# Two linear-attention blocks with a gate: the normalised numerator computed token-major and transposed, in place of a feature-major numerator with an expanded reciprocal

## Chip, cores and metric

One core of one Trainium2 chip runs the whole kernel. The metric is the device time of one execution in microseconds; the time before is the median of four runs. The profile is of one further execution, whose span (first to last instruction) is a little shorter than the device time.

## What is computed

Two linear-attention blocks, A and B, read the same input `x` of 2048 tokens by 640 features, with their own weights. There are 32 heads of 20 features. A sigmoid gate per token mixes the two results. Cut to what matters:

```python
# for each block, S = 2048, D = 640, H = 32, Dh = 20
qkv = x @ wqkv                              # 640 -> 3 * 640
phi = lambda t: where(t > 0, t + 1, exp(t)) + 1e-6
pq, pk = phi(q), phi(k)
kv  = einsum("bhsd,bhse->bhde", pk, v)      # per head 20 x 20, over all tokens
z   = einsum("bhsd->bhd", pk)
num = einsum("bhqd,bhde->bhqe", pq, kv)
den = einsum("bhqd,bhd->bhq", pq, z)
o   = num / den
block = o.reshape(B, S, D) @ wo
# the whole
g = sigmoid((x * gate_w).sum(-1))
out = g * A + (1 - g) * B
```

## The kernel before

Names: `P` = 128, `ST` = 16 token tiles of 128, `NS` = 4 groups of 512 tokens, `NQ` = 4 tiles in a group, `NCH` = 512, `DT` = `QT` = 5 feature tiles of 128. All tiles in PSUM come from one pool of eight one-bank buffers; `work` is a pool of two buffers per tag. The gate is multiplied into the reciprocals of the denominators, so that the last projection can add A and B in one accumulation. A matmul's `lhsT` is the stationary operand, its `rhs` the moving one; the contraction runs over partitions.

The queries are computed feature-major (`pqT`: features on partitions, tokens in the free dimension), the keys and values token-major:

```python
def q_group(blk, m, n):          # 128 features x 512 tokens
    pq_ps = ps_tile(f"pq_{blk}")
    for c in range(DT):
        nc.tensor.matmul(pq_ps[:, :NCH], lhsT=Wr[:, c, ...], rhs=xT[:, c, n * NCH:(n + 1) * NCH], ...)
    nc.scalar.activation(out=e[:], in_=pq_ps[:, :NCH], func=ACT.Exp)
    nc.scalar.activation(out=r[:], in_=pq_ps[:, :NCH], func=ACT.Relu)
    nc.vector.scalar_tensor_tensor(out=pqT[:, m, n * NCH:(n + 1) * NCH], in0=e[:], scalar=1.0, in1=r[:], op0=ALU.min, op1=ALU.add)

def kv_chunk(blk, i, with_gate):  # 128 tokens; three PSUM banks p0, p1, p2 of 512, 448 and 320 columns
    for pt, w, off in regions:
        for c in range(DT):
            nc.tensor.matmul(pt[:, :w], lhsT=xT[:, c, sl], rhs=Wr[:, c, off:off + w], ...)
    # ScalarE: Exp of p0 and of 128 columns of p1
    # VectorE: max(., 0) + 1e-6 of the same (kr), then min(e, 1) + r into pk
    # ScalarE: the values from p1 and p2 into vaug
```

`phase_kvwin` contracts `pk` with `vaug` over all tokens and leaves `KVbd`, the per-head 20 x 20 matrices on the diagonal of a 640 x 640 matrix. `den_group` gives the denominators token-major (128 tokens x 32 heads), `rec_ops` their reciprocals times the gate (`recs`). The part that the change replaces makes the reciprocals feature-major by a transpose and an expansion from 32 heads to 640 features with the 0/1 matrix `E`:

```python
def transposes(self, n):         # in RecState
    pr = ps_tile_bf16(f"recT_{self.blk}")
    for q in range(NQ):
        nc.tensor.transpose(out=pr[:H, q * P:(q + 1) * P], in_=self.recs[:, n * NQ + q, :], identity=identb[:])
    nc.vector.tensor_copy(out=self.recT[:H, n * NCH:(n + 1) * NCH], in_=pr[:H, :NCH])

def num_group(blk, oT, recT, j, n):   # 128 features x 512 tokens
    dch = echunks[j]                  # 2 or 3 feature tiles that meet the heads of tile j: 2, 3, 3, 3, 2
    for kk, c in enumerate(dch):
        nc.tensor.matmul(pn[:, :NCH], lhsT=KVbd[:, c, j * P:(j + 1) * P], rhs=pqT[:, c, n * NCH:(n + 1) * NCH], ...)
    nc.tensor.matmul(pr[:, :NCH], lhsT=E[:, j * P:(j + 1) * P], rhs=recT[:, n * NCH:(n + 1) * NCH], start=True, stop=True)
    nc.scalar.copy(out=numsb[:], in_=pn[:, :NCH])
    nc.vector.tensor_tensor(out=oT[:, j, n * NCH:(n + 1) * NCH], in0=numsb[:], in1=pr[:, :NCH], op=ALU.mult)

def final_group(i):                   # 128 tokens: ten stationary tiles (five of oTA, five of oTB), two banks of 320 columns
    for kk, (oT, wo, j) in enumerate(steps):
        nc.tensor.matmul(o0[:, :FH], lhsT=oT[:, j, sl], rhs=wo[:, j, 0:FH], ...)
        nc.tensor.matmul(o1[:, :FH], lhsT=oT[:, j, sl], rhs=wo[:, j, FH:D], ...)
    # ScalarE copies o0, VectorE o1, then the output DMA
```

The order of the whole is: q and kv of A interleaved; `KVbd`, denominators and reciprocals of A; four kv chunks of B; all transposes and numerators of A; q and kv of B interleaved; `KVbd`, denominators of B (three groups of 512 tokens); the last five q groups of B; numerators of B for group 0; then for each group of 512 tokens its B numerators (from group 1 on) and its four output chunks. Tile's scheduler may draw ready instructions ahead.

Of the kernel before, what the change touches and what calls it, by code (L numbers as in the profile page):

```python
# [8 lines left out]
P = 128  # L9
FP32 = mybir.dt.float32  # L10
BF16 = mybir.dt.bfloat16
ACT = mybir.ActivationFunctionType
ALU = mybir.AluOpType
# [3 lines left out]
def kernel(  # L17
# [11 lines left out]
    nc = tc.nc  # L29
# [3 lines left out]
    S, D = x2.shape  # L33
    H = 32
    Dh = D // H
    assert D % H == 0 and D % P == 0 and S % P == 0
    DT = D // P
    ST = S // P
    NCH = min(512, S)
    assert S % NCH == 0 and NCH % P == 0  # L40
    NS = S // NCH
    NQ = NCH // P
    QT = D // P
# [19 lines left out]
    for c in range(DT):  # L63
        h_lo = (c * P) // Dh
        h_hi = ((c + 1) * P - 1) // Dh
# [7 lines left out]
    echunks = []  # L73
# [7 lines left out]
    persist = ctx.enter_context(tc.tile_pool(name="persist", bufs=1))  # L81
    consts = ctx.enter_context(tc.tile_pool(name="consts", bufs=1))
    work = ctx.enter_context(tc.tile_pool(name="work", bufs=2))
    psum = ctx.enter_context(tc.tile_pool(name="psum", bufs=8, space=bass.MemoryType.PSUM))

    def ps_tile_bf16(name):
        return psum.tile([P, 2 * NCH], BF16, tag="ps", name=name)

    def ps_tile(name):
        return ps_tile_bf16(name).bitcast(FP32)  # L90
# [5 lines left out]
    pqT = persist.tile([P, QT, S], BF16, name="pqT")  # L96
    pk = persist.tile([P, ST, D], BF16, name="pk")
    vaug = persist.tile([P, ST, VAUG_W], BF16, name="vaug")
    oTA = persist.tile([P, QT, S], BF16, name="oTA")
    oTB = persist.tile([P, QT, S], BF16, name="oTB")  # L100
    KVbd = persist.tile([P, DT, D], BF16, name="KVbd")
    ZselA = persist.tile([P, DT, H], BF16, name="ZselA")
    ZselB = persist.tile([P, DT, H], BF16, name="ZselB")
    recTA = persist.tile([P, S], BF16, name="recTA")
    recTB = persist.tile([P, S], BF16, name="recTB")
    recsA = persist.tile([P, ST, H], BF16, name="recsA")
    recsB = persist.tile([P, ST, H], BF16, name="recsB")

# [10 lines left out]
        out=E[:H], in_=E[:H], pattern=[[-1, D]], compare_op=ALU.is_ge, fill=0.0, base=Dh - 1,  # L119
        channel_multiplier=Dh,  # L120
    )
    nc.vector.memset(recTA[:], 0.0)
    nc.vector.memset(recTB[:], 0.0)
    nc.gpsimd.memset(  # L124
        vaug[:].rearrange("p i (h t) -> p i h t", t=Dh + 1)[:, :, :, Dh:Dh + 1], 1.0
    )
# [60 lines left out]
    def q_group(blk, m, n):  # L187
        pq_ps = ps_tile(f"pq_{blk}")
        for c in range(DT):
            nc.tensor.matmul(  # L190
                pq_ps[:, :NCH],
                lhsT=Wr[:, c, OFF_Q + m * P:OFF_Q + (m + 1) * P],
                rhs=xT[:, c, n * NCH:(n + 1) * NCH],
                start=(c == 0), stop=(c == DT - 1),
            )
        e = work.tile([P, NCH], BF16, tag="qe", name="qe")
        r = work.tile([P, NCH], BF16, tag="qr", name="qr")
        nc.scalar.activation(out=e[:], in_=pq_ps[:, :NCH], func=ACT.Exp)  # L198
        nc.scalar.activation(out=r[:], in_=pq_ps[:, :NCH], func=ACT.Relu)  # L199
        nc.vector.scalar_tensor_tensor(  # L200
            out=pqT[:, m, n * NCH:(n + 1) * NCH], in0=e[:], scalar=1.0, in1=r[:],
            op0=ALU.min, op1=ALU.add,
        )

    def kv_chunk(blk, i, with_gate: bool):
        nB = K1_W + V0_W
        nC = V1_W + (1 if with_gate else 0)
        sl = slice(i * P, (i + 1) * P)
        p0 = ps_tile(f"p0_{blk}")
        p1 = ps_tile(f"p1_{blk}")  # L210
        p2 = ps_tile(f"p2_{blk}")
        regions = [(p0, K0_W, OFF_K0), (p1, nB, OFF_K1), (p2, nC, OFF_V1)]
        for pt, w, off in regions:
            for c in range(DT):
                first, last = (c == 0), (c == DT - 1)
                nc.tensor.matmul(pt[:, :w], lhsT=xT[:, c, sl], rhs=Wr[:, c, off:off + w], start=first, stop=last)  # L216
        e = work.tile([P, D], BF16, tag="ke", name="ke")
        r = work.tile([P, D], BF16, tag="kr", name="kr")
        nc.scalar.activation(out=e[:, 0:K0_W], in_=p0[:, 0:K0_W], func=ACT.Exp)  # L219
        nc.scalar.activation(out=e[:, K0_W:D], in_=p1[:, 0:K1_W], func=ACT.Exp)  # L220
        nc.vector.tensor_scalar(r[:, 0:K0_W], p0[:, 0:K0_W], 0.0, 1e-6, op0=ALU.max, op1=ALU.add)
        nc.vector.tensor_scalar(r[:, K0_W:D], p1[:, 0:K1_W], 0.0, 1e-6, op0=ALU.max, op1=ALU.add)
        nc.vector.scalar_tensor_tensor(  # L223
            out=pk[:, i, :], in0=e[:], scalar=1.0, in1=r[:], op0=ALU.min, op1=ALU.add,
        )
        nc.scalar.copy(
            out=vaug[:, i, 0:VSPLIT_H * (Dh + 1)].rearrange("p (h t) -> p h t", t=Dh + 1)[:, :, 0:Dh],
            in_=p1[:, K1_W:K1_W + V0_W].rearrange("p (h t) -> p h t", t=Dh),
        )
        nc.scalar.copy(  # L230
            out=vaug[:, i, VSPLIT_H * (Dh + 1):VAUG_W].rearrange("p (h t) -> p h t", t=Dh + 1)[:, :, 0:Dh],
            in_=p2[:, 0:V1_W].rearrange("p (h t) -> p h t", t=Dh),
        )
        if with_gate:
            nc.scalar.activation(out=gexp[:, i:i + 1], in_=p2[:, nC - 1:nC], func=ACT.Exp, scale=-1.0)
# [31 lines left out]

    class RecState:

        def __init__(self, blk, Zsel, gc, recs, recT):  # L270
            self.blk = blk
            self.Zsel = Zsel
            self.gc = gc
            self.recs = recs
            self.recT = recT
            self.den_tiles = [ps_tile(f"den{n}_{blk}") for n in range(NS)]

        def den_group(self, i):
# [16 lines left out]
                op=ALU.mult,  # L295
            )

        def transposes(self, n):
            pr = ps_tile_bf16(f"recT_{self.blk}")
            for q in range(NQ):  # L300
                i = n * NQ + q
                nc.tensor.transpose(out=pr[:H, q * P:(q + 1) * P], in_=self.recs[:, i, :], identity=identb[:])
            nc.vector.tensor_copy(out=self.recT[:H, n * NCH:(n + 1) * NCH], in_=pr[:H, :NCH])

    def num_group(blk, oT, recT, j, n):
        dch = echunks[j]
        pn = ps_tile(f"num_{blk}")
        pr = ps_tile(f"rt_{blk}")
        for kk, c in enumerate(dch):
            nc.tensor.matmul(  # L310
                pn[:, :NCH], lhsT=KVbd[:, c, j * P:(j + 1) * P], rhs=pqT[:, c, n * NCH:(n + 1) * NCH],
                start=(kk == 0), stop=(kk == len(dch) - 1),
            )
        nc.tensor.matmul(  # L314
            pr[:, :NCH], lhsT=E[:, j * P:(j + 1) * P], rhs=recT[:, n * NCH:(n + 1) * NCH],
            start=True, stop=True,
        )
        numsb = work.tile([P, NCH], BF16, tag="numsb", name="numsb")
        nc.scalar.copy(out=numsb[:], in_=pn[:, :NCH])  # L319
        nc.vector.tensor_tensor(  # L320
            out=oT[:, j, n * NCH:(n + 1) * NCH], in0=numsb[:], in1=pr[:, :NCH], op=ALU.mult,
        )

    FH = D // 2

    def final_group(i):
        sl = slice(i * P, (i + 1) * P)
        o0 = ps_tile("o0")
        o1 = ps_tile("o1")
        steps = [(oTA, woA, j) for j in range(QT)] + [(oTB, woB, j) for j in range(QT)]  # L330
        for kk, (oT, wo, j) in enumerate(steps):
            first, last = (kk == 0), (kk == len(steps) - 1)
            nc.tensor.matmul(o0[:, :FH], lhsT=oT[:, j, sl], rhs=wo[:, j, 0:FH], start=first, stop=last)  # L333
            nc.tensor.matmul(o1[:, :FH], lhsT=oT[:, j, sl], rhs=wo[:, j, FH:D], start=first, stop=last)  # L334
        osb = work.tile([P, D], BF16, tag="osb", name="osb")
        nc.scalar.copy(out=osb[:, 0:FH], in_=o0[:, :FH])  # L336
        nc.vector.tensor_copy(out=osb[:, FH:D], in_=o1[:, :FH])  # L337
        nc.sync.dma_start(out=out2[sl, :], in_=osb[:])
# [21 lines left out]
            kv_chunk("A", arg, True)  # L360
    phase_gate()
    phase_kvwin("A", ZselA)
    recA = RecState("A", ZselA, gcol, recsA, recTA)
    for i in range(ST):
        recA.den_group(i)
    for n in range(NS):
# [3 lines left out]
    LEAD_KV = min(ST, 4)  # L370
    for i in range(LEAD_KV):
        kv_chunk("B", i, False)
    for n in range(NS):
        recA.transposes(n)
    for n in range(NS):
        for j in range(QT):
            num_group("A", oTA, recTA, j, n)
    q_items_B = [("q", (n, m)) for n in range(NS - 1) for m in range(QT)]
    kv_items_B = [("kv", i) for i in range(LEAD_KV, ST)]
    for kind, arg in interleave(kv_items_B, q_items_B):  # L380
        if kind == "q":
            q_group("B", arg[1], arg[0])
        else:
            kv_chunk("B", arg, False)
    phase_kvwin("B", ZselB)
    recB = RecState("B", ZselB, gcolB, recsB, recTB)
    for i in range((NS - 1) * NQ):
        recB.den_group(i)
    for n in range(NS - 1):
        recB.rec_ops(n)  # L390
    for m in range(QT):
        q_group("B", m, NS - 1)
    for n in range(NS - 1):
        recB.transposes(n)
    if NS > 1:
        for j in range(QT):
            num_group("B", oTB, recTB, j, 0)
    for i in range((NS - 1) * NQ, ST):
        recB.den_group(i)
    recB.rec_ops(NS - 1)  # L400
    for n in range(NS):
        if n == NS - 1:
            recB.transposes(n)
        if n > 0 or NS == 1:
            for j in range(QT):
                num_group("B", oTB, recTB, j, n)
        for q in range(NQ):
            final_group(n * NQ + q)


# [28 lines left out]
```

## Time and profile before

| | before |
|---|---|
| device time, median of 4 runs | 241.11 us (240.51 to 242.0) |
| span of the profiled execution | 239.3 us |
| TensorE busy | 227.0 us, 95% |
| VectorE busy | 137.1 us, 57% |
| ScalarE busy | 127.7 us, 53% |
| matmuls | 1511 |

How to read it: matmuls are pipelined, so the duration of one (379 ns for 512 columns) is longer than the distance from one start to the next. The cost of a matmul in a row of matmuls is that distance, which the chain of work that ended last shows by its merged pieces. Idle time of an engine that is not the bottleneck costs nothing. Line numbers such as L310 are those of the kernel; L310 are the numerator matmuls, L314 the expansion of the reciprocal, L302 the transposes of the reciprocals.

### The profile page before, as it was taken

What the parts mean: (1) busy time and instruction counts of PE and PEld (TensorE: products, weight loads), DVE (VectorE), ACT (ScalarE), POOL (GpSimd) and SP (SyncE); (2) the same over time, 40 slices, a digit from 0 to 9 for tenths busy, and PEclk for the clock granted to TensorE, in tenths of its full rate; (3) what the DMA queues carried; (4) which work ended last, traced back from release to release, by engine and by line L of the source; (5) the groups of instructions that cost most, each with busy time, mean ns of one, the idle gap of its engine ahead of it and who ended that gap; (6) DMA issues with size and microseconds to landing.
All of it is one profiled execution on the core that took longest, in us unless ns stands there. A gap on an engine that the chain in (4) does not pass through costs nothing.

```text
span 239.3 us, 3842 instructions
## 1 busy us (share of the span) xinstructions
PE 227.0 (95%) x1511; PEld 129.5 (54%) x1511; DVE 137.1 (57%) x256; ACT 127.7 (53%) x281; POOL 8.0 (3%) x12
## 2 busy tenths in 40 slices
PE   0599999999999999999999999999999999999994
PEld 0235555455555975544554555559547657576572
DVE  3456656575657488888665656564884252432511
ACT  2047676867776326677668677763581242421410
POOL 8400000000000000000000000000000000000000
PEclk9999999999999999999999999999999999999999
DMA  6999700000000910000000000000000101101011
GB/s 186 187 283 198 272 0 1 1 3 0 0 0 9 358 49 0 3 0 1 0 4 0 0 0 3 0 0 3 0 4 27 55 30 55 55 30 55 27 56 58
DMA packets 18786, 12.05 MB, mean 50 GB/s; under 512 B 11600, under 2 KB 18768, under 8 KB 18768
## 3 DMA queue, kind: packets, MB, share of 16 engines
q1 hardware_dynamic: 18768, 11.80, 18.0%
q8 instruction: 12, 0.20, 0.3%
q14 instruction: 6, 0.05, 0.1%
HBM read 6.55 MB, written 2.62 MB: 38 GB/s over the span
## 4 chain that ended last, share of the span: by engine, by line
PE 94%; POOL 3%; DVE 1%; POOLq 0%; issue 0%; DVEq 0%
PE p_A L216 18%; PE p_B L216 18%; PE pq_A L190 10%; PE o L334 9%; PE o L333 9%; PE pq_B L190 9%; PE num_A L310 5%; PE num_B L310 5%; PE rt_B L314 2%; PE rt_A L314 2%; PE kva_A L249 1%; PE kva_B L249 1%; PE pb L184 1%; POOL KVbd L127 1%; POOL vaug L124 1%; PE kvb_B L249 1%
## 5 line engine op out<-in xcount | busy, mean ns | idle before, releaser
L216 PEld LDWEIGHTS <-xT 128*128 128x128 bf16 x480 | 46.7, 97 | 43.5
L200 DVE SCALAR_TENSOR_TENSOR pqT<-qe,qr 128x512 bf16<-128x512 bf16 x40 | 27.6, 690 | 40.7 <-ACT qr L199 40.7
L216 PE MATMUL p_B<-Wr,xT 128*128 128x512 bf16 (+2 forms) x240 | 45.7, 343 | 0.0
L216 PE MATMUL p_A<-Wr,xT 128*128 128x512 bf16 (+2 forms) x240 | 45.4, 344 | 0.0
L190 PEld LDWEIGHTS <-Wr 128*128 128x128 bf16 x200 | 19.9, 100 | 20.9 <-issue 2.9
L223 DVE SCALAR_TENSOR_TENSOR pk<-ke,kr 128x640 bf16<-128x640 bf16 x32 | 26.4, 824 | 1.1
L337 DVE CAST osb<-o 128x320 bf16<-128x320 f32 x16 | 7.9, 491 | 32.7 <-PE o L334 30.1
L336 ACT CAST osb<-o 128x320 bf16<-128x320 f32 x16 | 6.8, 425 | 37.0 <-PE o L333 37.0
L190 PE MATMUL pq_A<-xT,Wr 128*128 128x512 bf16 x100 | 25.5, 400 | 0.0
L190 PE MATMUL pq_B<-xT,Wr 128*128 128x512 bf16 x100 | 24.0, 379 | 0.0
L333 PE MATMUL o<-woB,oTB 128*128 128x320 bf16 x80 | 22.2, 299 | 0.0
L334 PE MATMUL o<-woA,oTA 128*128 128x320 bf16 x80 | 22.2, 299 | 0.0
L334 PE MATMUL o<-woB,oTB 128*128 128x320 bf16 x80 | 22.2, 299 | 0.0
L333 PE MATMUL o<-woA,oTA 128*128 128x320 bf16 x80 | 22.2, 299 | 0.0
L198 ACT ACTIVATE qe<-pq_A 128x512 bf16<-128x512 f32 x20 | 11.9, 597 | 16.7 <-PE pq_A L190 16.7
L198 ACT ACTIVATE qe<-pq_B 128x512 bf16<-128x512 f32 x20 | 11.9, 597 | 11.5 <-PE pq_B L190 11.5
L310 PEld LDWEIGHTS <-KVbd 128*128 128x128 bf16 x104 | 9.9, 98 | 11.3
L320 DVE TENSOR_TENSOR oTB<-numsb,rt_B 128x512 bf16<-128x512 bf16 x20 | 13.5, 685 | 3.8 <-ACT numsb L319 3.1
L320 DVE TENSOR_TENSOR oTA<-numsb,rt_A 128x512 bf16<-128x512 bf16 x20 | 13.6, 687 | 2.0 <-ACT numsb L319 0.9
L310 PE MATMUL num_B<-pqT,KVbd 128*128 128x512 bf16 x52 | 14.5, 379 | 0.0
L310 PE MATMUL num_A<-pqT,KVbd 128*128 128x512 bf16 x52 | 14.5, 379 | 0.0
L219 ACT ACTIVATE ke<-p_B 128x512 bf16<-128x512 f32 x16 | 9.6, 597 | 9.1 <-PE p_B L216 9.1
(73 smaller groups left out, 254.3 us busy)
## 6 DMA issues: line engine op xcount, KB each, us to landing
out_dram<-osb SPq DMA_DIRECT2D x16, 160.0 KB, 1.8
Wr<-in_A_wqkv_dram SPq DMA_DIRECT2D x3, 800.0 KB, 6.1
Wr<-in_B_wqkv_dram SPq DMA_DIRECT2D x3, 800.0 KB, 6.3
woA<-in_A_wo_dram SPq DMA_DIRECT2D x1, 800.0 KB, 5.9
woB<-in_B_wo_dram SPq DMA_DIRECT2D x1, 800.0 KB, 7.4
xT<-in_A_x_dram SPq DMA_TRANSPOSE x10, 4.2
Wr<-in_gate_w_dram SPq DMA_DIRECT2D x1, 1.2 KB, 7.7
```

What stands on the lines that cost most here:

```text
L190: nc.tensor.matmul(pq_ps[:, :NCH], lhsT=Wr[:, c, OFF_Q + m * P:OFF_Q + (m + 1) * P], rhs=xT[:, c, n * NCH:(n + 1) * NCH], start=(c == 0), ...
L198: nc.scalar.activation(out=e[:], in_=pq_ps[:, :NCH], func=ACT.Exp)
L200: nc.vector.scalar_tensor_tensor(out=pqT[:, m, n * NCH:(n + 1) * NCH], in0=e[:], scalar=1.0, in1=r[:], op0=ALU.min, op1=ALU.add,)
L216: nc.tensor.matmul(pt[:, :w], lhsT=xT[:, c, sl], rhs=Wr[:, c, off:off + w], start=first, stop=last)
L219: nc.scalar.activation(out=e[:, 0:K0_W], in_=p0[:, 0:K0_W], func=ACT.Exp)
L223: nc.vector.scalar_tensor_tensor(out=pk[:, i, :], in0=e[:], scalar=1.0, in1=r[:], op0=ALU.min, op1=ALU.add,)
L310: nc.tensor.matmul(pn[:, :NCH], lhsT=KVbd[:, c, j * P:(j + 1) * P], rhs=pqT[:, c, n * NCH:(n + 1) * NCH], start=(kk == 0), stop=(kk == len ...
L314: nc.tensor.matmul(pr[:, :NCH], lhsT=E[:, j * P:(j + 1) * P], rhs=recT[:, n * NCH:(n + 1) * NCH], start=True, stop=True,)
L320: nc.vector.tensor_tensor(out=oT[:, j, n * NCH:(n + 1) * NCH], in0=numsb[:], in1=pr[:, :NCH], op=ALU.mult,)
L333: nc.tensor.matmul(o0[:, :FH], lhsT=oT[:, j, sl], rhs=wo[:, j, 0:FH], start=first, stop=last)
L334: nc.tensor.matmul(o1[:, :FH], lhsT=oT[:, j, sl], rhs=wo[:, j, FH:D], start=first, stop=last)
L337: nc.vector.tensor_copy(out=osb[:, FH:D], in_=o1[:, :FH])
```

## The change

The numerator is computed token-major, like the denominator: a 128-token tile of `pqT` becomes the stationary operand and the columns of `KVbd` that belong to its heads move through. Six pieces per chunk, of 140, 140, 80, 80, 140 and 140 columns, fill two banks of 320 columns (16 heads each). The reciprocal then has the same layout, tokens on partitions and heads in the free dimension, and is applied while the bank is evicted, by a multiplication that broadcasts it over the 20 features of a head. Neither the transposed reciprocal nor its expansion is needed any more. The result `oN` is token-major, and the output projection wants features on partitions, so it is transposed on TensorE, 20 transposes for 512 tokens, and copied out of PSUM by ScalarE and VectorE in turn.

The order changes too: eight of B's kv chunks are put between the chunks of A's numerator, one after every second; B's first chunks are put between the last q groups; and each output chunk of one group of 512 tokens follows a numerator chunk of the next group.

The diff, cut to its core:

```diff
-    recTA = persist.tile([P, S], BF16, name="recTA")
-    recTB = persist.tile([P, S], BF16, name="recTB")
...
-    nc.vector.memset(recTA[:], 0.0)
-    nc.vector.memset(recTB[:], 0.0)
...
-        def transposes(self, n): ...
-    def num_group(blk, oT, recT, j, n): ...
...
+    # o_pieces: [c, u, v, bank, start, stop], columns u:v of feature tile c; a window that crosses FH = 320 is cut there
+    def o_chunk(blk, i, recs, oN):
+        q = i % NQ
+        po = [ps_tile(f"o0_{blk}"), ps_tile(f"o1_{blk}")]
+        lhsT = pqT[:, :, i * P:(i + 1) * P]
+        for (c, u, v, bank, st, sp) in o_pieces:
+            base = 0 if bank == 0 else FH
+            nc.tensor.matmul(
+                po[bank][:, u - base:v - base], lhsT=lhsT[:, c], rhs=KVbd[:, c, u:v], start=st, stop=sp,
+                skip_group_check=True,
+            )
+        nh0 = FH // Dh
+        nc.vector.tensor_tensor(
+            out=oN[:, q, 0:FH].rearrange("p (h t) -> p h t", t=Dh),
+            in0=po[0][:, 0:FH].rearrange("p (h t) -> p h t", t=Dh),
+            in1=recs[:, i, 0:nh0, None].to_broadcast([P, nh0, Dh]),
+            op=ALU.mult,
+        )
+        nc.vector.tensor_tensor(   # the same for columns FH:D from po[1]
...
+    def o_transposes(blk, n, oN, oT):
+        for j in range(QT):
+            pt = ps_tile_bf16(f"oT_{blk}")
+            for q in range(NQ):
+                nc.tensor.transpose(
+                    out=pt[:, q * P:(q + 1) * P], in_=oN[:, q, j * P:(j + 1) * P], identity=identb[:],
+                )
+            if j % 2 == 0:
+                nc.scalar.copy(out=oT[:, j, n * NCH:(n + 1) * NCH], in_=pt[:, :NCH])
+            else:
+                nc.vector.tensor_copy(out=oT[:, j, n * NCH:(n + 1) * NCH], in_=pt[:, :NCH])
...
     for i in range(LEAD_KV):
         kv_chunk("B", i, False)
+    kv_next = LEAD_KV
     for n in range(NS):
-        recA.transposes(n)
-    for n in range(NS):
-        for j in range(QT):
-            num_group("A", oTA, recTA, j, n)
+        oN = work.tile([P, NQ, D], BF16, tag="oN", name="oN")
+        for q in range(NQ):
+            o_chunk("A", n * NQ + q, recsA, oN)
+            if q % 2 == 1:
+                kv_chunk("B", kv_next, False)
+                kv_next += 1
+        o_transposes("A", n, oN, oTA)
...
+    oN = work.tile([P, NQ, D], BF16, tag="oN", name="oN")
     for m in range(QT):
+        if m < NQ:
+            o_chunk("B", m, recsB, oN)
         q_group("B", m, NS - 1)
-    for n in range(NS - 1):
-        recB.transposes(n)
-    if NS > 1:
-        for j in range(QT):
-            num_group("B", oTB, recTB, j, 0)
+    o_transposes("B", 0, oN, oTB)
     for i in range((NS - 1) * NQ, ST):
         recB.den_group(i)
     recB.rec_ops(NS - 1)
     for n in range(NS):
-        if n == NS - 1:
-            recB.transposes(n)
-        if n > 0 or NS == 1:
-            for j in range(QT):
-                num_group("B", oTB, recTB, j, n)
+        if n + 1 < NS:
+            oN = work.tile([P, NQ, D], BF16, tag="oN", name="oN")
         for q in range(NQ):
+            if n + 1 < NS:
+                o_chunk("B", (n + 1) * NQ + q, recsB, oN)
             final_group(n * NQ + q)
+        if n + 1 < NS:
+            o_transposes("B", n + 1, oN, oTB)
```

More of the change, by code (lines that the diff above doesn't have):

```diff
@@ L268, with __init__ @@
     class RecState:
-        def __init__(self, blk, Zsel, gc, recs, recT):
+        def __init__(self, blk, Zsel, gc, recs):
             self.blk = blk
@@ L274, in __init__ @@
             self.recs = recs
-            self.recT = recT
             self.den_tiles = [ps_tile(f"den{n}_{blk}") for n in range(NS)]
@@ L296, in rec_ops @@
             )
-        def transposes(self, n):
-            pr = ps_tile_bf16(f"recT_{self.blk}")
-            for q in range(NQ):
[L301 to L322, printed above, removed]
@@ L324 @@
-    FH = D // 2
+    FH = (H // 2) * Dh
+    assert FH % Dh == 0
+    o_pieces = []
+    prev_hi = 0
+    bank_started = [False, False]
+    for c in range(DT):
+        h_lo = (c * P) // Dh
+        h_hi = ((c + 1) * P - 1) // Dh
+        lo, hi = h_lo * Dh, (h_hi + 1) * Dh
+        ranges = [(lo, hi)]
+        for (a, b) in ranges:
+            for (u, v) in ((a, min(b, FH)), (max(a, FH), b)):
+                if u < v:
+                    bank = 0 if u < FH else 1
+                    o_pieces.append([c, u, v, bank, not bank_started[bank], False])
+                    bank_started[bank] = True
+        prev_hi = hi
@@ new lines @@
+    assert prev_hi == D
+    for bank in range(2):
+        idxs = [k for k, pc in enumerate(o_pieces) if pc[3] == bank]
+        o_pieces[idxs[-1]][5] = True
+    def o_chunk(blk, i, recs, oN):
[16 more added lines that the diff above has]
+        nc.vector.tensor_tensor(
+            out=oN[:, q, FH:D].rearrange("p (h t) -> p h t", t=Dh),
+            in0=po[1][:, 0:D - FH].rearrange("p (h t) -> p h t", t=Dh),
+            in1=recs[:, i, nh0:H, None].to_broadcast([P, H - nh0, Dh]),
+            op=ALU.mult,
+        )
@@ new lines, in o_transposes @@
+    def o_transposes(blk, n, oN, oT):
+        for j in range(QT):
+            pt = ps_tile_bf16(f"oT_{blk}")
+            for q in range(NQ):
+                nc.tensor.transpose(
+                    out=pt[:, q * P:(q + 1) * P], in_=oN[:, q, j * P:(j + 1) * P], identity=identb[:],
+                )
+            if j % 2 == 0:
+                nc.scalar.copy(out=oT[:, j, n * NCH:(n + 1) * NCH], in_=pt[:, :NCH])
+            else:
+                nc.vector.tensor_copy(out=oT[:, j, n * NCH:(n + 1) * NCH], in_=pt[:, :NCH])
@@ L326, in final_group, with o_block @@
+    def o_block(blk, n, recs, oT):
+        oN = work.tile([P, NQ, D], BF16, tag="oN", name="oN")
+        for q in range(NQ):
+            o_chunk(blk, n * NQ + q, recs, oN)
+        o_transposes(blk, n, oN, oT)
     def final_group(i):
@@ L362 @@
     phase_kvwin("A", ZselA)
-    recA = RecState("A", ZselA, gcol, recsA, recTA)
+    recA = RecState("A", ZselA, gcol, recsA)
     for i in range(ST):
@@ L372 @@
         kv_chunk("B", i, False)
+    kv_next = LEAD_KV
     for n in range(NS):
-        recA.transposes(n)
-    for n in range(NS):
-        for j in range(QT):
-            num_group("A", oTA, recTA, j, n)
+        oN = work.tile([P, NQ, D], BF16, tag="oN", name="oN")
[5 more added lines that the diff above has]
+        o_transposes("A", n, oN, oTA)
     q_items_B = [("q", (n, m)) for n in range(NS - 1) for m in range(QT)]
-    kv_items_B = [("kv", i) for i in range(LEAD_KV, ST)]
+    kv_items_B = [("kv", i) for i in range(kv_next, ST)]
     for kind, arg in interleave(kv_items_B, q_items_B):
@@ L385 @@
     phase_kvwin("B", ZselB)
-    recB = RecState("B", ZselB, gcolB, recsB, recTB)
+    recB = RecState("B", ZselB, gcolB, recsB)
     for i in range((NS - 1) * NQ):
@@ L401 @@
     for n in range(NS):
-        if n == NS - 1:
-            recB.transposes(n)
-        if n > 0 or NS == 1:
-            for j in range(QT):
-                num_group("B", oTB, recTB, j, n)
+        if n + 1 < NS:
+            oN = work.tile([P, NQ, D], BF16, tag="oN", name="oN")
         for q in range(NQ):
+            if n + 1 < NS:
+                o_chunk("B", (n + 1) * NQ + q, recsB, oN)
             final_group(n * NQ + q)
+        if n + 1 < NS:
+            o_transposes("B", n + 1, oN, oTB)
 _INS = ['A_x', 'A_wqkv', 'A_wo', 'B_x', 'B_wqkv', 'B_wo', 'gate_w']
```

## The prediction

> **What bounds the kernel now.** I read the page first: busy time per engine, then the slices, then the chain that ended last.
>
> ```profile
> PE 227.0 (95%) x1511; PEld 129.5 (54%) x1511; DVE 137.1 (57%) x256; ACT 127.7 (53%) x281; POOL 8.0 (3%) x12
> ...
> PEclk9999999999999999999999999999999999999999
> ...
> PE 94%; POOL 3%; DVE 1%; POOLq 0%; issue 0%; DVEq 0%
> ```
>
> The reader is to see one bound: TensorE (PE) holds 94% of the chain, at full clock in every slice. Nothing else is near it on average, so what counts is TensorE time added and removed, and whether another engine becomes the bound inside a stage. The next view is the chain in order of time, for the A numerator stage and the work around it.
>
> ```profile
> 82.10 2.08 PE kvb_A L249 x32
> ...
> 85.02 1.60 PE den_A L281 x64
> 86.62 10.41 PE p_B L216 x58
> 97.03 1.00 PE recT_A L302 x16
> 98.03 0.54 PE num_A L310 x2
> 98.56 0.22 PE rt_A L314
> 98.78 0.65 PE num_A L310 x3
> ...
> 113.46 0.22 PE rt_A L314
> 113.67 2.71 PE p_B L216 x15
> ```
>
> Columns: start, length, instructions. These rows are my price list, because a matmul's own duration (379 ns at 512 columns) overlaps with the next; the step is what it costs. A 512-column matmul steps 0.65/3 = 0.216 us, a 147-column one 2.08/32 = 0.065, a 32-column one 1.60/64 = 0.025, a 128-column transpose 1.00/16 = 0.062. A key and value chunk (p_B, 15 matmuls) takes 2.71. All of these except the rt matmul load a new 128-column stationary operand (the transpose one of 32 columns), so weight loads are already inside these steps: at 0.025 us they do not show.
>
> The stage windows (length, then each engine's busy time) and the groups that the change replaces or copies:
>
> ```profile
> 97.03:113.67 16.64, 16.64 (x89) 7.98 (x90) 14.60 (x24) 12.05 (x22) 0.00 (x0) 1.00 0.01 1
> ...
> 162.37:174.69 12.32, 12.32 (x167) 9.07 (x165) 8.38 (x21) 5.46 (x11) 0.00 (x0) 1.00 0.00 1
> ```
>
> ```profile
> L319 ACT CAST numsb<-num_A 128x512 bf16<-128x512 f32 x20 | 11.7, 585 | 4.6 <-PE num_A L310 3.8 <-DVE oTA L320 0.5
> ...
> L337 DVE CAST osb<-o 128x320 bf16<-128x320 f32 x16 | 7.9, 491 | 32.7 <-PE o L334 30.1 <-ACT osb L336 2.6
> ...
> L303 DVE COPY recTA<-recT_A 32x512 bf16<-32x512 bf16 x4 | 1.4, 403 | 0.0
> ...
> L261 DVE TENSOR_TENSOR KVbd<-kva_A,BD 128x140 bf16<-128x140 f32 x2 | 0.6, 296 | 0.0
> ```
>
> In the A numerator window TensorE is fully busy, VectorE 14.60 of 16.64 us, ScalarE 12.05. VectorE has little room in this stage even now.
>
> **What the Trainium skill says.** "TensorE: Matmul & The Clock Gate", section "Wait — 56ns, not 53.3ns?", gives start-to-start as N/2.4 GHz plus about 2.5 ns at full clock: 216 ns for 512 columns, 56 for 128. The trace agrees: 0.216, and 0.065 at 147 columns where the rule says 0.064. The same page, section "Back-to-back issue gap", says that streams of weight load and matmul sustain only about 81 ns at 128 columns; this trace contradicts it, since 147 columns with a fresh weight load each step 65 ns. I price by the trace. "VectorE: DVE Perf Modes", section "The perf-mode tier table", puts a two-tensor operation with a PSUM operand at one element per cycle and a copy from PSUM at up to two. The trace agrees: 296 ns for the 140-element product from PSUM, 403 for the 512-element bf16 copy against 685 for the 512-element product. "PSUM — Partial Sum Buffer", section "Specifications (TRN2)", gives eight banks per partition; the kernel's PSUM pool has eight one-bank buffers, and the trace of before shows no wait for one among its longer waits.
>
> **The change part by part.**
>
> Removed on TensorE, per block: 52 numerator matmuls and 20 expansions of the reciprocal, all of 512 columns, and 16 transposes of reciprocals. For A this is 97.03 to 113.67, 16.64 us. For B the chain has four pieces: 174.69 to 179.47 (4.78), 190.83 to 194.72 (3.89), 205.59 to 209.46 (3.87), and the last from about 220.35 to 224.92 (4.57), in which TensorE also waits some 0.6 us for the copy of the transposed reciprocals (recTB). Together 17.1; both blocks 33.75 us.
>
> Added on TensorE, per 128-token chunk: six matmuls with a pqT tile as stationary operand, whose column windows follow the heads: 140, 140, 80, 80, 140, 140. From the 0.065 step less 2.9 ns per seven columns I put 140 columns at 0.062 and 80 at 0.037, so 4 x 0.062 + 2 x 0.037 = 0.322 us. Two blocks of 16 chunks: 32 x 0.322 = 10.3. This is where the saving comes from: the numerator streamed 13 x 512 columns per 512 tokens and the expansion 5 x 512, 9,216 in all; now it is 4 x 720 = 2,880. Then 20 transposes per 512 tokens, 160 in all; I take 0.060, between the 0.062 read above and the page's 0.056: 9.6. Sum added 19.9.
>
> TensorE alone: 33.75 - 19.9 = 13.9 us less, 241.1 - 13.9 = 227.2.
>
> Moved: VectorE now evicts the numerator itself, two products of 320 elements per chunk (485 to 490 ns each, from the 491 of the osb eviction of the same size), and ScalarE's 585 ns numerator casts go. The transposed result is evicted by copies, three by ScalarE (585) and two by VectorE (403). Also, eight B key and value chunks are moved in between A's chunks. For 512 tokens of A, TensorE takes 4 x 0.322 + 2 x 2.71 + 20 x 0.060 = 7.9 us. VectorE takes 8 x 0.49 for the products, 2 x (0.686 + 0.282 + 0.824) for the two key chunks, 2 x 0.403 for copies: 3.9 + 3.6 + 0.8 = 8.3 by durations. But VectorE's instructions overlap at their ends: in the timeline a 686 ns operation of the key chunk is followed after 0.61. Taking 0.07 off each of the products, and about that off some others, gives about 7.5. So VectorE is at 95 to 100% of TensorE's pace for 32 us. ScalarE has 2 x 1.74 + 3 x 0.585 = 5.2, no bound.
>
> Near balance with chained waits does not run without gaps. At the end of each 512 tokens, five PSUM buffers hold transposes, the next two chunks want four, and only three are free until a copy is done; ScalarE's copies queue behind value casts, which wait for VectorE. Working one period through by hand, the second chunk of the next period waits 0.2 to 0.5 us. I charge 0.35 x 4 = 1.4 us.
>
> B's entry: three denominators' reciprocals keep VectorE busy about 3.5 us (168.96 to 172.4 in the timeline), and four chunks of products (8 x 0.42 = 3.4) plus five q operations (0.69 each, 3.4) follow. TensorE has only five q groups of 1.08 and four chunks of 0.322, 6.7 us from about 169.7, so it reaches the transposes near 176.4, while VectorE has evicted the fourth chunk near 177.5. Up to 1.1 us of wait, partly filled if the next chunks are scheduled ahead; I charge 0.6. In the later B stages VectorE has half its time free, and each transpose stage is followed by ten A matmuls of the output projection (1.36 us), which cover its copies: nothing charged. The two VectorE memsets at the start lie off the chain, which there runs through POOL: nothing gained.
>
> Sum: 227.2 + 1.4 + 0.6 = 229.2; I say 229.
>
> **The rivals.** First, **weight loads come to light**: a weight load is recorded at 97 ns, and 192 short matmuls and 160 transposes at 97 each make 34.1 us against 33.75 removed, so about 241.5 and no change. For it speaks that 80 columns stream in less time than a load lasts, and the skill's 81 ns; against it, the denominator's 0.025 us steps with full-width loads. I give it little. Second, **VectorE becomes the bound of the A stage**: if its durations add without overlap and chained waits leave gaps of 10%, a period is 9.1 us and not 7.9, which costs 4.9 and ends near 233. For it speaks 8.3 against 7.9; against it, the overlap seen and the quieter q stage behind, in which VectorE catches up. Third, **TensorE alone**: buffers hide all of it and the schedule fills B's entry, 227; transposes at 0.056 would then give 226.6. In before, VectorE ran at 88% in that same stage without stopping TensorE.
>
> **Range and chances.** The centre is TensorE's sum plus 2 us of waits. Below it lie the 2 us of waits not occurring and 0.6 from the transposes; above it the second rival's 4 us. So 225.5 to 233.5. Faster by over 2% means under 236.3: to miss it, waits of over 9 us or the first rival are needed; I give faster 0.94, same 0.05, slower 0.01.
>
> **What would show it.** In the profile after, the chain should still be some 90% TensorE; six-matmul chunks should step about 0.32 us and twenty transposes 1.2; the products should be near 490 ns and alternate with key operations, with VectorE over 90% busy in a window some 33 us long from 97; small TensorE waits should be charged to VectorE or ScalarE evictions at the boundaries of the 512 tokens, about 0.35 each. The prediction is wrong if transposes or short matmuls step near 97 ns, if the products with a broadcast operand take much more than 490, or if the A stage with its eight key chunks takes over 36 us.

## The result, and the profile after

The changed kernel takes 227.57 us (median of ten runs, 226.88 to 228.22) against 241.43 for the kernel before: a ratio of 0.943, 95% interval 0.9413 to 0.9448. The prediction said 229.0, and 225.5 to 233.5 as the range.

The page of the changed kernel: busy times, the granted clock, the chain that ended last by engine.

```profile
PE 213.4 (94%) x1687; PEld 133.4 (59%) x1687; DVE 137.2 (61%) x286; ACT 116.1 (51%) x265; POOL 8.0 (4%) x12
...
PEclk9999999999999999999999999999999999999999
...
PE 90%; DVE 3%; POOL 3%; ACT 1%; POOLq 0%; issue 0%; DVEq 0%; ACTq 0%
```

TensorE is still the bound, with 176 more matmuls in 13.6 us less busy time. Some of the chain has gone to VectorE and ScalarE (3% and 1%), and the rest of this page is about where. The same chain in order of time, through one group of 512 tokens of A:

```profile
97.55 0.63 PE o_A L321 x12
98.18 2.71 PE p_B L212 x15
100.89 0.63 PE o_A L321 x12
101.52 2.71 PE p_B L212 x15
104.23 1.12 PE oT_A L343 x20
105.34 0.63 PE o_A L321 x12
```

Every piece starts where the last one ended: two numerator chunks 0.63 us (0.315 each), twenty transposes 1.12 (0.056 each), no gap at the boundary from transposes to the next chunks. The windows of the changed kernel, A's numerator stage and then B's entry (length, then the busy time of TensorE, weight loads, VectorE, ScalarE, GpSimd):

```profile
97.55:128.73 31.18, 31.18 (x297) 21.12 (x295) 29.52 (x65) 18.55 (x44) 0.00 (x0) 1.00 0.01 2
...
161.07:172.07 11.00, 10.89 (x151) 7.33 (x147) 10.51 (x25) 6.66 (x13) 0.00 (x0) 1.00 0.01 1
```

A's stage is TensorE from end to end, although VectorE is busy for 95% of it. At B's entry VectorE is busy for 96% and the chain runs through it:

```profile
161.93 0.41 PE den_B L276 x16
...
162.35 1.77 DVE rcp L285 x2
...
164.38 0.95 DVE rcp L285
165.33 0.34 DVE oN L326
...
165.87 0.40 DVE oN L332
166.27 0.60 DVE pqT L196
```

To compare kernels without the start, I take two stretches from the first start of the matmuls that contract keys and values (kva): A's, from kva_A to kva_B, holds A's numerators and all of B's projections but the last five q groups; B's runs from kva_B to the end of the span.

| | A's stretch | B's stretch | span |
|---|---|---|---|
| before | 83.5 | 77.1 | 239.3 |
| changed | 76.4 | 70.3 | 225.9 |
| 1 new arithmetic, old order | 82.7 | 75.6 | 237.5 |
| 2 old arithmetic, new order | 83.5 | 83.4 | 245.1 |
| 3 the change in A alone | 76.4 | 78.1 | 232.7 |
| 4 copies on VectorE | 76.8 | 70.5 | 226.8 |
| 5 copies on ScalarE | 77.1 | 70.1 | 226.4 |
| 6 numerator pieces twice | 81.4 | 75.1 | 235.2 |
| 7 transposes twice | 80.8 | 74.6 | 233.6 |
| 8 reciprocals later | 76.3 | 69.9 | 225.9 |
| 9 old arithmetic, new order in A | 83.5 | 77.1 | 239.5 |
| 10 as 8, memsets moved | 76.4 | 69.6 | 223.5 |

The change saves 7.1 us in A's stretch and 6.8 in B's. The start gave none of it: kva_A begins at 78.7 us before and 79.2 after, and between 78.2 and 79.7 in other runs whose start is that of one of these two (the last section says what moves it). B's stretch ends with the last output's eviction and transfer, which lie behind TensorE's last matmul: 3.5 to 3.9 us in these executions, but 4.6 in run 3. Up to the start of that matmul B takes 73.28 us before and 66.32 changed.

### The profile page after: what moved, and what is told of

Same layout as the page of the kernel before. It is cut to its first block, busy times and chain, and to the rows that moved or that the text cites. A ratio compares the mean times of both kernels' runs of the same rounds, so it can differ in the third digit from the quotient of the medians.

```text
span 225.9 us, 4153 instructions
## 1 busy us (share of the span) xinstructions
PE 213.4 (94%) x1687; PEld 133.4 (59%) x1687; DVE 137.2 (61%) x286; ACT 116.1 (51%) x265; POOL 8.0 (4%) x12
## 4 chain that ended last, share of the span: by engine, by line
PE 90%; DVE 3%; POOL 3%; ACT 1%; POOLq 0%; issue 0%; DVEq 0%; ACTq 0%
PE p_A L212 19%; PE p_B L212 19%; PE pq_A L186 11%; PE o L364 10%; PE o L365 10%; PE pq_B L186 7%; PE o_A L321 2%; PE oT_A L343 2%; PE o_B L321 2%; PE oT_B L343 1%; PE kva_B L245 1%; PE kva_A L245 1%; PE pb L180 1%; DVE rcp L285 1%; POOL KVbd L123 1%; POOL vaug L120 1%
## 5 line engine op out<-in xcount | busy, mean ns | idle before, releaser
L186 PE MATMUL pq_A<-xT,Wr 128*128 128x512 bf16 x100 | 26.0, 406 | 0.0
L186 PE MATMUL pq_B<-xT,Wr 128*128 128x512 bf16 x100 | 23.0, 379 | 0.0
L364 PE MATMUL o<-woA,oTA 128*128 128x320 bf16 x80 | 21.8, 299 | 0.1
L365 PE MATMUL o<-woA,oTA 128*128 128x320 bf16 x80 | 21.8, 299 | 0.0
L194 ACT ACTIVATE qe<-pq_B 128x512 bf16<-128x512 f32 x20 | 11.9, 597 | 10.2 <-DVE rcp L285 7.3
L217 DVE TENSOR_SCALAR kr<-p_B 128x512 bf16<-128x512 f32 x16 | 11.0, 689 | 4.3 <-ACT ke L215 4.3
L217 DVE TENSOR_SCALAR kr<-p_A 128x512 bf16<-128x512 f32 x16 | 11.0, 686 | 3.9 <-ACT ke L215 3.9
L321 PEld LDWEIGHTS <-pqT 128*128 128x128 bf16 x192 | 11.6, 98 | 1.8
L195 ACT ACTIVATE qr<-pq_A 128x512 bf16<-128x512 f32 x20 | 11.8, 592 | 0.0
L195 ACT ACTIVATE qr<-pq_B 128x512 bf16<-128x512 f32 x20 | 11.8, 591 | 0.0
```

The lines of the kernel that those rows point to most:

```text
L186: nc.tensor.matmul(pq_ps[:, :NCH], lhsT=Wr[:, c, OFF_Q + m * P:OFF_Q + (m + 1) * P], rhs=xT[:, c, n * NCH:(n + 1) * NCH], start=(c == 0), ...
L321: nc.tensor.matmul(po[bank][:, u - base:v - base], lhsT=lhsT[:, c], rhs=KVbd[:, c, u:v], start=st, stop=sp, skip_group_check=True,)
```

## The experiments

The theory after the result: TensorE's sum sets the time, and the new order is what lets it, by putting other matmuls beside the evictions. The rivals: the arithmetic alone brings the gain; the order alone brings it; VectorE's near balance costs something in A.

**1. The changed arithmetic in the order of before.**

```diff
     for n in range(NS):
-        oN = ...; for q: o_chunk("A", ...); after every second one kv_chunk("B", kv_next, False)
-        o_transposes("A", n, oN, oTA)
+        o_block("A", n, recsA, oTA)          # four chunks, then their transposes
 ...
     for m in range(QT):
-        if m < NQ: o_chunk("B", m, recsB, oN)
         q_group("B", m, NS - 1)
-    o_transposes("B", 0, oN, oTB)
+    o_block("B", 0, recsB, oTB)
 ...                                          # and o_block("B", n, ...) ahead of each group's outputs
```

> The changed arithmetic in the order of before: all of A's numerator in one stretch, each B numerator group in one stretch ahead of its four output chunks. Theory (TensorE's saving is paid out only because the new order puts other matmuls beside the evictions): VectorE needs about 8 x 0.40 + 2 x 0.35 = 3.9 us for 512 tokens and TensorE only 4 x 0.315 + 1.12 = 2.4, so TensorE waits about 1.5 us in each of A's four groups and up to 2.4 us in each of B's; 235 to 241 us. Rival (the arithmetic alone brings the gain, buffers and the scheduler hide the evictions): 226.5 to 229.

Measured: 239.3 us, ratio to the kernel before 0.9918 (0.9892 to 0.9944). The new arithmetic by itself brings about 2 of the 13.9 us. Its chain in A's numerator stage:

```profile
98.36 0.40 DVE oN L326
...
101.15 0.40 DVE oN L332
101.54 0.80 DVE oTA L349 x2
...
111.90 0.41 DVE oN L326
112.36 0.40 PE oT_A L343 x4
```

Not one TensorE piece stands in it for 14 us: eight products at 0.40 and two copies, 3.98 us for 512 tokens, where TensorE has 2.4 us of work. The stage's window says the same, VectorE 15.77 of 15.80 us:

```profile
97.30:113.10 15.80, 14.60 (x174) 9.93 (x173) 15.77 (x41) 5.44 (x11) 0.00 (x0) 1.00 0.01 2
```

Here the page's average misleads: VectorE is 58% busy over the span and is the bound of this stage. TensorE's "busy" 14.60 is no evidence against it either; that count includes short matmuls whose records reach over the waits (a transpose is recorded at 219 ns and steps 56). The stage took 16.64 us before, so TensorE's saving turned into a wait for VectorE. In B each group's transposes wait in the same manner (B's stretch is 75.6).

**2. The arithmetic of before in the new order.**

```diff
         for j in range(QT):
             num_group("A", oTA, recTA, j, n)
+            if j == 1 or j == 3: kv_chunk("B", kv_next, False)   # eight in all
 ...
     for m in range(QT):
         q_group("B", m, NS - 1)
+        if m == 0: recB.transposes(0)
+        num_group("B", oTB, recTB, m, 0)
 ...                                          # and B's later numerators between the output chunks
```

> The arithmetic of before in the order of the change. Theory (TensorE was already busy through A's numerator, so the order alone has nothing to fill but the 0.6 us wait for the last transposed reciprocals): 240 to 241.5 us. Rival (the interleaving itself brings a good part of the gain): under 237.

Measured: 248.34 us, ratio 1.0292 (1.0224 to 1.0361): slower, which no theory had. That is a median between two pairs of executions, 246.8 and 247.0 us at a mean granted clock of 0.993 and 249.7 and 249.9 at 0.986; the profile is of the first pair. A's stretch is as before (83.5), so the loss lies in B. The chain there, two cuts:

```profile
168.47 1.77 DVE rcp L290 x2
...
172.19 0.33 DVE recTB L303
172.56 0.38 PE rt_B L314
...
180.86 0.41 DVE recTB L303
...
182.80 0.88 DVE rcp L290
...
184.05 0.40 PE recT_B L302 x4
```

The old numerator needs the reciprocal on TensorE, transposed and expanded, and put this early it waits for VectorE's reciprocals twice, about 1.7 and 2.2 us. After the second wait the clock falls; the windows of that stretch end with the granted clock before the last two columns:

```profile
180.50:184.40 3.90, 1.66 (x33) 1.25 (x34) 3.10 (x6) 0.95 (x2) 0.00 (x0) 1.00 0.00 0
184.40:190.00 5.60, 5.60 (x27) 3.24 (x27) 1.48 (x3) 1.01 (x2) 0.00 (x0) 0.70 0.00 0
```

By the distances between its matmuls TensorE loses some 6.7 us between 160 and 192 us, of which about 1.6 lie in the stretch at the lower clock; in the kernel of before it loses about 0.7 in the whole of B. So my order for B differs in what it makes TensorE wait for, and this run mixed two things. Run 9 separates them for A.

**9. The arithmetic of before, the new order in A alone.** The edit is the first part of the one above; B is as before.

> The arithmetic of before with the new order in A alone (eight of B's key and value chunks between A's numerators); B is exactly as before. It separates the order of A from that of B, which the run with both mixed. Theory (no gap to fill in A): the same as before, 240.5 to 242 us. Rival (the interleaving of A is worth something by itself): under 239.

Measured: 241.08 us, ratio 0.9997 (0.9983 to 1.0011), A's stretch 83.5 as before. With TensorE busy all the time, there was nothing for the order to fill. Together with run 1: in A, the arithmetic alone brings 0.8 us, the order alone nothing, both 7.1. In B the arithmetic alone brings 1.5 us and both 6.8; what the order alone would bring there without waits of its own is not shown.

**3. The change in A alone.** RecState.transposes, num_group and recTB are kept for B, and B's part of the program is that of before.

> Only block A has the token-major numerator and the new order; B is as before. Theory (the gain is TensorE's sum, stage by stage): A saves 16.64 - 16 x 0.315 - 80 x 0.056 = 7.1 us, so 234.3 us, give or take 0.7, and B's part, the rest to 227.6, is 6.7. Rival (VectorE's near balance in A's stage costs there what B's gains): 236 or more.

Measured: 235.44 us, ratio 0.9753 (0.9718 to 0.9788), above the expected 234.3, give or take 0.7, and below the rival's 236. The profiled execution (234.45 us) shows A's stretch at 76.4, the same 7.1 us less as in the whole change. B's stretch is 1.0 longer than before, but not by TensorE: up to its last matmul B takes 73.28 us as before, and the 1.0 lies behind it. The near balance costs A nothing.

**4. All five copies of the transposed result on VectorE.**

```diff
-            if j % 2 == 0:
+            if False:
                 nc.scalar.copy(out=oT[...], in_=pt[:, :NCH])
             else:
                 nc.vector.tensor_copy(out=oT[...], in_=pt[:, :NCH])
```

> All five copies of the transposed result on VectorE. VectorE's starts in the changed A stage add up to 7.2 of 7.79 us for 512 tokens; three more copies of 0.35 make 8.3. Theory (VectorE has about 0.5 us to spare in 7.8 and bounds beyond it): the A stage grows by 0.5 us for each 512 tokens, 2 us in all, 229 to 230.5 us. Rival (the durations added without overlap, 8.0 before and 9.2 with them, are what counts): 5 us more, 232 or above. Third (waits are hidden anyway): 227.6.

Measured: 228.45 us, ratio 0.9466 (0.944 to 0.9492), 0.9 us over the changed kernel and not 2. Two cuts of the chain, at the first and the last boundary at which TensorE waits:

```profile
112.35 0.24 PE oT_A L343 x4
112.61 0.42 DVE oTA L349
113.03 0.73 DVE pk L219
113.76 1.33 DVE oTA L349 x4
...
120.62 0.42 DVE oTA L349
121.05 0.73 DVE pk L219
121.78 0.35 DVE oTA L349
122.16 2.87 PE p_B L212 x15
```

VectorE is now the bound there: 8.01 us from one boundary to the next (112.61 to 120.62). But the stage, from its first chunk to the next key chunk behind it (97.87 to 129.49), is only 31.62 us, 0.44 more than 31.18; another 0.4 comes in B (66.69 us up to the last matmul, against 66.32). The expectation had VectorE's slack wrong. Five copies of 0.35 give a back-to-back period of 8.01 us, so with two copies VectorE needs 6.96 of the 7.79, and its slack is 0.8 us and not 0.5. The three further copies exceed it by 0.2 and not by 0.5. TensorE waits 0.22 us at two of the boundaries, and each wait ends with VectorE's second copy: the key chunk (p_B) starts at 114.15 and 122.16, 0.05 us after that copy's end (114.10, 122.11). The key chunk reads nothing of oTA, so what it waits for is the PSUM buffer. At the first boundary there is no wait yet, and what VectorE owes at the end is paid in the q stage, where it has room.

**5. All five on ScalarE** (the same line with `if True:`).

> All five copies of the transposed result on ScalarE, so VectorE has 0.7 us less in 512 tokens. Theory (in the changed kernel TensorE never waits in A's stage, so a relieved VectorE gives nothing there; only B's entry, where both copies stand behind VectorE's reciprocals, could gain some tenths): 227 to 228.3 us. Rival (VectorE's near balance costs the 1.4 us that the prediction charged): 226.2 or less. Other way to fail: ScalarE's five copies of about 0.5 become the last to end before the next output chunks: 229 or more.

Measured: 227.87 us, ratio 0.9435 (0.9418 to 0.9452): no gain, as expected, but A's stretch is 0.7 longer. The chain at the first boundary, and at the last:

```profile
104.25 0.43 ACT vaug L222
...
105.01 2.32 ACT oTA L347 x5
107.38 0.61 ACT ke L215
108.00 0.69 DVE kr L217
...
121.04 0.99 ACT oTA L347 x2
122.07 2.87 PE p_B L212 x15
```

The chain runs through ScalarE, although that is only 66% busy in the stage (20.79 of 31.37 us). TensorE loses 0.22 us at each of the three boundaries, and again for a PSUM buffer: the key chunk starts 0.05 us after the end of ScalarE's second copy (106.04 after 105.99, 114.05 after 114.00, 122.07 after 122.02). With the copies split three and two, ScalarE and VectorE make the first two side by side, done at 105.49 us, and the key chunk starts at 105.81 without a wait. The exponential behind the five copies is not what comes late: it starts 1.34 us after the key chunk in the changed kernel and here.

**6. Numerator pieces twice, 7. transposes twice.**

```diff
-        for (c, u, v, bank, st, sp) in o_pieces:
+        for (c, u, v, bank, st, sp) in o_pieces + o_pieces:        # run 6
 ...
-            for q in range(NQ):
+            for q in list(range(NQ)) + list(range(NQ)):            # run 7
                 nc.tensor.transpose(...)
```

> Each numerator chunk's six matmuls are issued twice into the same banks (the second pass starts the banks anew, so the result is that of one pass). It prices the short matmuls on the path: theory (each chunk steps 0.315 us, weight loads hidden, TensorE bound everywhere but at B's entry): 32 x 0.315 = 10.1 us more, less the 0.7 us of waits that they fill at B's entry: 236.5 to 238 us. Rival (a stationary operand is not loaded in time for an 80-column matmul, 97 ns each): 192 x 0.097 = 18.6 us more, 246. Rival (TensorE has slack in A's stage): clearly under 236.

> Each of the 160 transposes is issued twice to the same place. Theory (0.056 us each on the path): 9.0 us more, 235.5 to 237 us. Rival (transposes of a full 128-column stationary operand lie near the 0.081 that the skill gives for weight-load streams): 13 us more, 240 or above. Rival (transposes stand where TensorE would wait anyway): under 234.

Measured: 237.2 us, ratio 0.9826 (0.9809 to 0.9842), and 235.89, ratio 0.9779 (0.9758 to 0.9801): 9.6 and 8.3 us more than the changed kernel. A's stretch grows by 5.0 (16 x 0.315) and 4.4 (80 x 0.056 = 4.5). A line of the chain of each, two chunks with doubled pieces in run 6 and the doubled transposes of 512 tokens in run 7:

```profile
97.00 1.26 PE o_A L321 x24
...
103.21 2.23 PE oT_A L343 x40
```

Both prices are those of the steps, on the path, with a fresh full-width weight load each time. That settles the first rival of the prediction (97 ns each): it is out.

**8. Reciprocals later at B's entry.**

```diff
-    for i in range((NS - 1) * NQ): recB.den_group(i)
-    for n in range(NS - 1): recB.rec_ops(n)
+    for i in range(NQ): recB.den_group(i)
+    recB.rec_ops(0)
 ...                                          # q groups and first chunks of B
+    for i in range(NQ, (NS - 1) * NQ): recB.den_group(i)
     o_transposes("B", 0, oN, oTB)
+    for n in range(1, NS - 1): recB.rec_ops(n)
```

> At B's entry only the first 512 tokens' denominators and reciprocals come ahead of the first numerator chunks; those of the second and third 512 tokens follow the last q groups. Theory (B's entry waits for VectorE, which first does 2.7 us of reciprocals; TensorE's work there is 10.2 of 11.0 us): the wait goes, 226.6 to 227.2 us. Rival (the wait moves: the denominators' banks or the later reciprocals hold up the second group instead): 227.6 or more.

Measured: 226.88 us, ratio 0.9397 (0.9376 to 0.9417). Its chain at B's entry has TensorE again:

```profile
163.53 0.32 PE o_B L321 x6
163.84 1.08 PE pq_B L186 x5
...
166.63 2.16 PE pq_B L186 x10
168.79 0.99 PE den_B L276 x40
169.78 1.13 PE oT_B L343 x20
```

B's stretch is 0.4 us shorter (65.84 us up to the last matmul, against 66.32). The interval touches that of the changed kernel, so the gain of the median, 0.7, is not secured by this run alone; that most of the wait went is seen in the chain.

**10. The same with a shorter start.** The page puts 3% of the chain on GpSimd: its memsets of vaug (2.30 us) and KVbd (2.71) stand before the selects of E for which TensorE's first matmul waits until 8.7 us.

```diff
-    nc.gpsimd.memset(vaug[...][:, :, :, Dh:Dh + 1], 1.0)
-    nc.gpsimd.memset(KVbd[:], 0.0)
+    nc.vector.memset(vaug[...][:, :, :, Dh:Dh + 1], 1.0)
+    nc.vector.memset(KVbd[:], 0.0)
```

> The version with the later reciprocals, and the two memsets that stand before E's selects on GpSimd (vaug, KVbd; 5.0 us of the first 8.7 that TensorE waits) on VectorE, which the change has freed at the start. Theory (GpSimd's chain holds TensorE until 8.72 us): the setup matmuls start 4 to 5 us earlier, and the first q group as soon as x has landed; 223.5 to 225.5 us. Rival (the transposing loads of x set the first q group at 11.9 us anyway): 226.5 to 227.

Measured: 225.77 us, ratio 0.9379 (0.9354 to 0.9404), the lowest median here; its interval lies below that of the changed kernel, but overlaps that of run 8, from which it differs by the memsets alone (1.1 us by the medians). Of 4.6 us by which the setup matmuls start earlier, 1.7 arrive at kva_A (77.5 against 79.2), because another wait takes over:

```profile
4.08 0.20 PE L175 MATMUL pm<-identb,E 32*128 32x32 bf16 x1 [4.08 <-POOL E L116]
...
7.33 1.04 PE L186 MATMUL pq_A<-xT,Wr 128*128 128x512 bf16 x2
...
10.89 0.59 PE L186 MATMUL pq_A<-xT,Wr 128*128 128x512 bf16 x1 [1.17 <-DMA xT<-in_A_x_dram]
...
11.93 6.13 PE L186 MATMUL pq_A<-xT,Wr 128*128 128x512 bf16 x21 [0.45 <-DMA xT<-in_A_x_dram]
```

The first q group now waits for the transposing loads of x. Of the 1.7 us about 0.9 need not be the memsets' doing: the full clock began 1.74 us earlier in this execution (see the last section), well within what other kernels show from one execution to the next. That leaves about 0.9 us, near the 1.1 of the medians. The rival was right about what comes next and the theory about GpSimd's wait, but both ranges missed: 225.77 lies just above the theory's and below the rival's.

## Why the prediction was right, point by point

- **TensorE bounds, and its sum decides.** Right. The removed 33.75 us stand. The added part was 10.1 + 9.0 = 19.1 and not 19.9: a chunk steps 0.315 (said 0.322), a transpose 0.056 (said 0.060). The Trainium skill, page "TensorE: Matmul & The Clock Gate", section "Wait — 56ns, not 53.3ns?", has 0.056 for 128 columns, which the trace confirms; I had taken the mean of a row that also held waiting at its ends. The 81 ns of its section "Back-to-back issue gap" is contradicted by runs 6 and 7.
- **The A stage's waits, 1.4 us.** The mis-sized term: they are zero, and the sign that was named for them, waits of about 0.35 at the boundaries, is absent. The mechanism (banks held by transposes until copied) exists: in runs 4 and 5 the key chunk waits 0.22 us for the second copy. In the changed kernel that copy comes in time. VectorE reaches its first copy at 104.99 us, 0.35 before the transposes' end (105.34), and the second bank is free 0.3 us before the key chunk wants it (105.49 against 105.81). The prediction put VectorE at 95 to 100% of TensorE's pace. By durations that was right (29.52 of 31.18); in starts it is 6.96 of 7.79 us for 512 tokens (run 4), 89%, so there are 0.8 us of slack. A product steps 0.40 where the estimate had 0.42, and a key chunk's three operations take 1.53 us back to back (run 4) where their durations add up to 1.79.
- **B's entry, 0.6 us.** Right in place and near in size: the TensorE work there adds up to about 10.2 us by steps (64 denominators at 0.025, five chunks at 0.315, five q groups at 1.08, the transposes, four output matmuls at 0.136) in 11.0. Run 8 took about 0.5 of the 0.8 out.
- **The rivals.** Weight loads: out (runs 6, 7). VectorE as the bound of A: not in this order, but exactly so in the old one (run 1), which the prediction did not ask. TensorE alone: the nearest, 226.6 with the cheaper transposes, plus B's entry.
- **Two readings.** The prediction read "full clock in every slice" from the row of nines; at the start of the kernel that row holds no measurement (see the last section). And the expansion's matmul loads a new 128-column stationary operand too (40 weight loads from E for its 40 matmuls), so it is no exception in the price list. Neither changes a sum.
- **What it did not weigh.** It priced the order only as something moved. The order is worth most of the gain: 241.43 to 239.3 without it, to 227.57 with it. In its total the prediction came out right because it worked out VectorE against TensorE in the new order, and not because TensorE's sum holds in any order.

With the measured terms the sum is 33.75 - 19.1 - 0.8 (B's entry) = 13.9 us, and 241.43 - 13.9 = 227.5, against 227.57 measured. Of the 2.2 us that the prediction charged too much, 1.4 are A's waits and 0.8 the cheaper matmuls. The rest, up to the 1.4 us between 229.0 and 227.57, is rounding, the base of 241.1 and 0.2 too little for B's entry.

## What to carry to other kernels

Work saved on the bounding engine is worth its time only if the stage it is saved in still holds enough of that engine's work beside the others' evictions: compare the engines stage by stage, in steps from start to start and not in recorded durations, and move independent matmuls into the stage before counting the gain. Apply a normalising factor at eviction rather than as an operand of the bounding engine: run 2 shows that a factor that must pass through TensorE can make TensorE wait for the engine that computes it. When a stage is near balance, buffers and a lighter stage behind it absorb a small deficit (run 4). What a copy costs the bounding engine depends on when it frees the buffer that is wanted next, and not only on its engine's load (run 5: ScalarE 66% busy, and TensorE waits).

## What was unexpected of the hardware

In run 2, two waits of about 1.7 and 2.2 us within 14 us of each other were followed by half of TensorE's rate: for some 3 us, 320-column output matmuls stepped 0.27 us instead of 0.136.

```profile
185.54 0.27 PE o L333
```

The granted clock was 0.70 over the 5.6 us shown with run 2, and 0.50 in the 3.41 us from 185.26. So a wait on the bounding engine can be followed by a loss of its own, here about 1.7 us; no run tests by itself that the waits caused it. The sum of the waits does not decide it: in A's stage of run 1 TensorE lacks work for over 6 us of 15.8 (3.98 us for 2.4 us of work, four times), in pieces of at most 0.4, and the clock there stayed 1.00; one gap of 0.95 us in that run's B (176.02 to 177.02) did not lower it either. How long a single wait must be, these runs do not tell.

The doubled step, 0.43 us for 512 columns, also stands at the start of the changed kernel, in its first ten matmuls of the q groups:

```profile
11.91 4.43 PE L186 MATMUL pq_A<-xT,Wr 128*128 128x512 bf16 x10
```

The trace has no granted clock for this time, and the views put 1.00 (a 9) in its place. Its record of the full clock begins at 16.62 us here, at 15.57 in the kernel before, and between 14.55 and 17.51 in the twelve profiled executions. Except in run 10, whose start differs, kva_A follows that moment at half its pace, since the steps before it take twice as long: 78.20 us for 14.55, 78.70 for 15.57, 79.22 for 16.62 and 79.66 for 17.51. So up to 1.5 us of a single execution's span come from when the full clock begins, and not from the kernel.
